# Weight transfers of the expert stage placed behind the second tile's row gathers, and a splitting step, a product and filler work moved to other points of the routing

## The chip, the cores and the metric

The kernel runs on one core of a Trainium2 chip. That core has a matrix engine (TensorE, PE in the profile; its weight loads are listed as PEld), a vector engine (VectorE, DVE), a scalar engine (ScalarE, ACT), a general engine (GpSimd, POOL) and a queue engine (SyncE, SP) that issues most transfers; 16 DMA engines move the data. The metric is device time in microseconds (us) for one execution. The kernel before takes 780.52 us (median of three runs, 780.04 to 780.82).

## The reference

Three layers follow each other. Attention with a threshold: scores below the row's maximum minus `tau` are dropped. Then a mixture of eight experts, one per token, where a token may take over the expert of the token ahead of it. Then a second mixture of four attention experts with a causal mask.

```
scores = q @ k.T / 8; keep scores >= max - tau; x = softmax(scores) @ v          # 4 batches, 8 heads, 576 tokens
logits = x @ w_gate; local = sigmoid(x @ w_local)
for b, s:  e = argmax(logits[b, s]) if s == 0 or local[b, s] < 0.5 else prev_e   # a chain along the tokens
           out[b, s] = softmax(logits[b, s])[e] * (relu(x[b, s] @ w1[e]) @ w2[e])  # w1: 512x1024, w2: 1024x512
out2 = sum over the top 2 of 4 experts of weight * (causal attention of that expert)
```

The expert layer can't start on a token before the chain along all tokens of its batch is known, and rows are then gathered by expert into tiles of 256 or 352 tokens.

## The kernel before

Each engine executes its instructions in the order in which they were written; that order is made by hand. Stage 1 is the attention over 16 pairs of heads. Its order comes from a table of due times: `at(g, f)` puts step `f` at time `g`, where `g = 9 * p` for pair `p`, and the last pair has times of its own. Work of the next stage is hooked into the last pairs by the tables `EARLY` (routing of the first three batches), `TX0` (transposing the rows of the first expert tile) and `S0` (splitting its weights).

A split turns a 128x1024 piece of a weight matrix into a high part (`w1h`, `w2h`, by ACT, or by DVE for the pieces in `DVEH`) and a low part (`w1l`, `w2l`, the difference, by DVE or POOL), so that three matrix products of reduced precision make one of full precision. A tile's weights are eight pieces, 0 to 3 of `w1` and 4 to 7 of `w2`; two pieces come with each 1 MB transfer into a buffer `raw`.

`Route.main` follows stage 1. It ends the routing: a chain of small DVE steps and small matmuls over all tokens, with scans (L709, L713), the inverse list `inv` (L780) that says which row goes to which tile, and behind it the expert list `erow` (L798, L823) and the probability `psel` of the chosen expert (L825 to L837). While that chain runs, `fill(i)` gives PE `FILL[i]` pieces of the first expert tile's products: there are 32 pieces, 16 of the first product (six matmuls of 256 columns, L992) and 16 of the second (three matmuls of 512 columns, L1017). `flush` then writes the evacuations of finished accumulators.

After `inv`, POOL issues three row gathers for tile 1, the second tile (`first`, L1647). After the routing, `moe` resumes. It issues six weight transfers on SP (`load`, L909), each after reading the expert's number from `erow`; then for each of the three row blocks of tile 1 it runs pieces until `LEFT[i]` are left, transposes the block (`tx`, L961) and issues a gather for a later tile. Tile 1 uses the weights of tile 0, so the six transfers are for tile 2 and the first half of tile 3. The accumulator bank of the transpose of block 1 (`py`) stands where the routing had `po`, the product that selects the chosen expert's probability (L815, read at L833).

Of the kernel before, what the change touches and what calls it, by code (L numbers as in the profile page):

```python
# [9 lines left out]
F32 = mybir.dt.float32  # L10
# [3 lines left out]
I32 = mybir.dt.int32  # L14
AF = mybir.ActivationFunctionType
ALU = mybir.AluOpType
# [21 lines left out]
class Events:  # L38
# [4 lines left out]
    def at(self, g, pri, f, *a):  # L43
        self.n += 1
        self.ev.setdefault(g, []).append((pri, self.n, f, a))
# [53 lines left out]
class Consts:  # L99
# [5 lines left out]
    def load(self):  # L105
        self.nc.sync.dma_start(self.t, self.src)
# [6 lines left out]
def stage1(tc, nc, K, qT, qx, kT, vp, tau, wgl, x_dram, L, X, E2, hooks=(), npair=NP):  # L113
    ctx = ExitStack()
    C = ctx.enter_context(tc.tile_pool(name="s1c", bufs=1))
    P1 = ctx.enter_context(tc.tile_pool(name="s1", bufs=2))
    PS = ctx.enter_context(tc.tile_pool(name="s1p", bufs=1, space=PSUM))
    ident = K["ident"]
# [292 lines left out]
    for p in range(npair):  # L411
        g = 9 * p
        at(g - (27 if p < 2 else 21), load, p)
        at(g - (18 if p < 2 else 4.5), load_v, p)
        if p:
            at(g - 17, split_q, p)
        for a in range(2):
            if p:
                at(g - 9 + 2 * a, split_k, p, a)
                at(g - 8 + 2 * a, split_kl, p, a)  # L420
                at(g - 5 + a, split_ql, p, a)
            else:
                at(2 * a - 7, split_k, p, a)
                at(2 * a - 6, split_kl, p, a)
                at(a / 4 - 5.75, split_ql, p, a)
        at(g - 3.5, merge, p)
        for j in range(9):
            for n, f in (("S", scores), ("red", rowmax), ("tau", thresh), ("exp", expo), ("keep", keep), ("tp", tp), ("ev", tp_ev)):
                at(g + W[n][j], f, p, j)
        at(g + W["diag"], diag, p)  # L430
        T = W
        if p == npair - 1:
            T = dict(W, row=(11.3, 14.36), rev=(11.7, 14.7), recip=10.6)
            at(g + 13, norm_last)
            at(g + 14.71, logits_last)
            at(g + 14.75, norm_last)
        for h in range(2):
            at(g + T["tpm"][h], tpm, p, h)
            at(g + T["pmev"][h], tpm_ev, p, h)
            for k in range(5):  # L440
                at(g + T["av"][h], av, p, h, k)
            at(g + T["xt"][h], av_ev, p, h)
            at(g + T["row"][h], rows, p, h)
            at(g + T["rev"][h], rows_ev, p, h)
        at(g + T["keep"][8] + 0.1, sums, p)
        at(g + T["recip"], recip, p)
        if p < npair - 1:
            at(g + T["rev"][1] + 0.1, norm, p)
# [25 lines left out]
class Route:  # L474
# [201 lines left out]
    def main(self, fill, first):  # L676
# [6 lines left out]
        U, mx = self.U, self.mx  # L683
# [12 lines left out]
        def small(o, l, r, stop=True):  # L696
            mm(o, l, r, start=False, stop=stop, skip_group_check=True)
# [60 lines left out]
        pt = px[:, 276:336].rearrange("p (j g b) -> p j g b", j=5, g=3)  # L758
        for j in range(5):
            small(px[:, 276 + 12 * j:288 + 12 * j], O[:, 128 * j:128 * j + 128], sel2.rearrange("p g b -> p (g b)"))  # L760
        fill(6)
        ln3 = W.tile([128, 5, 128], F16, name="ln3")
        for j in range(5):
# [8 lines left out]
        r1 = W.tile([128, 20, NC], F16, name="r1")  # L772
        v.tensor_tensor(r1, K["iota"][:, 2:].unsqueeze(1).to_broadcast([128, 20, NC]),
                        col[:, 0].rearrange("p j b -> p (j b)").unsqueeze(2).to_broadcast([128, 20, NC]), op=ALU.is_equal)
        self.flush()
        pi = px[:, 340:340 + NC]
        for i in range(20):
# [15 lines left out]
        small(pe[:, 32:34], K["b0"][0:32], tf)  # L793
        fill(7)
        erow = C.tile([1, 2 * NT + 1], I32, name="erow")
        tot = W.tile([1, 2], F32, name="tot")
        fl = W.tile([1, NT + 1], F32, name="fl")
        v.tensor_scalar(erow[:, 0:NT], pe[:, 0:NT], 7.0, None, op0=ALU.min)  # L798
        v.tensor_copy(tot, pe[:, 32:34])
        for n, (o, w) in enumerate(((0, PMAX), (PMAX, LMAX))):  # L800
            v.tensor_scalar(fl[:, o:o + w], K["iota"][0:1, 0:w], tot[:, n:n + 1], None, op0=ALU.is_le)
# [7 lines left out]
        v.tensor_tensor(lt[:, 0], lt[:, 0], lt[:, 1], op=ALU.subtract)  # L809
        v.tensor_reduce(lt[:, 1, 0:1], lt[:, 0], axis=AX.X, op=ALU.max)  # L810
        small(pe[:, 40:41], lt[:, 1, 0:1], K["w8"][:, 7:8])

        po = PS.tile([128, 512], F32, name="po", tag="pa")[:, 0:160].rearrange("p (i e) -> p i e", e=8)
        for j in range(5):
            mm(po[:, 4 * j:4 * j + 4], O[:, 128 * j:128 * j + 128], K["ident"][0:32, 0:32],  # L815
               start=(j == 0), stop=(j == 4), skip_group_check=True)
        fill(8)
        self.flush()
        self.M.splits0()
        v.tensor_tensor(fl[:, NT:], fl[:, PMIN:PMIN + 1], fl[:, PMAX + LMIN:PMAX + LMIN + 1], op=ALU.max)  # L820
        v.tensor_tensor(fl[:, NT:], fl[:, NT:], pe[:, 40:41], op=ALU.add)
        v.tensor_scalar(fl[:, NT:], fl[:, NT:], 1.0, None, op0=ALU.min)
        v.tensor_copy(erow[:, NT:], fl)  # L823
        ex = W.tile([128, 20, 8], F32, name="ex")
        v.tensor_tensor(ex, L.rearrange("p j b n -> p (j b) n")[:, :, 0:8],  # L825
                        mx.rearrange("p j b -> p (j b)").unsqueeze(2).to_broadcast([128, 20, 8]), op=ALU.subtract)
        nc.scalar.activation(ex, ex, AF.Exp)
        den = W.tile([128, 20], F32, name="den")
        psel = C.tile([128, 20], F32, name="psel")
        v.tensor_reduce(den, ex, axis=AX.X, op=ALU.add)  # L830
# [6 lines left out]
            v.tensor_copy(psel[64:128, 16 + 2 * i:17 + 2 * i], psel[0:64, 17 + 2 * i:18 + 2 * i])  # L837
        ctx.close()
        self.slot, self.erow, self.psel = slot, erow, psel


def split_chunk(nc, W, src, t, c):
# [74 lines left out]
def moe(tc, nc, K, R, E, M, yg, W, ctx):  # L917
# [32 lines left out]
    def gather():  # L950
        if rows:
            M.fetch(rows.pop(0))
# [18 lines left out]
    def split(t, c):  # L971
        wc[t, c] = split_chunk(nc, E, R.piece(t, c), t, c)
# [73 lines left out]
    def lab(f, *a):  # L1046
        CUR[0] = f.__name__ + str(a)
        f(*a)
# [4 lines left out]
    def load():  # L1053
        if todo:
            load_w(*todo.pop(0))
# [33 lines left out]
                    yield  # L1089

    yield
    M.splits0 = lambda: split(0, 7)
    pieces = start()
    left = 32
    while not M.routed:
# [4 lines left out]
    P2.append(ctx.enter_context(tc.tile_pool(name="mop2", bufs=1, space=PSUM)))  # L1100
    M.last()
    ws, erow, fetch, fetch3, xscale = M.ws, M.erow, M.fetch, M.fetch3, M.xscale
    for _ in range(6):
        load()
    for i in range(3):
        while left > LEFT[i]:
            next(pieces)
            M.flush()
            left -= 1
        lab(tx, 1, i)  # L1110
        gather()
    for _ in pieces:
        M.flush()
    M.flush()
# [74 lines left out]
class Weights3:  # L1189
# [15 lines left out]
    def split(self, r, n, k):  # L1205
        self.nc.scalar.activation(self.h[n][:, k], r, AF.Copy)
        self.nc.vector.tensor_sub(self.l[n][:, k], r, self.h[n][:, k].bitcast(F32))


def stage3(tc, nc, K, ws, xr, fetch, xscale, row, out, nb=B):  # L1210
# [380 lines left out]
    for y in range(2 * nb):  # L1591
# [10 lines left out]
        for h, n in enumerate((5, 10)):  # L1602
# [6 lines left out]

FILL = (2, 1, 4, 2, 1, 1, 2, 3, 0)
EARLY = (60, 123.4, 123.42, 123.44, 123.46, 124.2, 124.25, (124.55, 125), (125.65, 126.1), (126.12, 126.4), 126.7, 127.2, 127.8, 128.4,
         (129.25, 129.55), 129.7, 129.9, (131.58, 131.95), 132, 133, 134.5, 136, 137.5, 139, (141.1, 141.4))
W0 = 129.8
R0 = 141.45
TX0 = ((146.85, 147.25), (147.7, 149.3))
S0 = ((138.5, 140), (140.3, 142), (144.7, 145.3), (147.4, 147.9), (147.5, 148.2), (147.6, 148.5), (148.8, 148.85))
LEFT = (16, 15, 14)
TL = 4  # L1620
POOL = ((0, 0), (0, 1))
DVEH = ((0, 6),)
# [6 lines left out]
def model(tc, cst, qT, qx, kT, vp, tau, wgl, w12, wqk, wv, wo, out):  # L1629
    nc = tc.nc  # L1630
    with ExitStack() as ctx:
# [6 lines left out]
        with ExitStack() as mx, ExitStack() as rx:  # L1638
# [41 lines left out]
                return f  # L1680

            hooks = [(27, lambda *_: R.clear(tc)), *zip(EARLY, rt.early()), (W0, weights0), (R0, rows0)]
            hooks += [*zip(TX0, (tx0(0), tx0(1))), *zip(S0, map(split0, range(7)))]
            stage1(tc, nc, K, qT, qx, kT, vp, tau, wgl, x_dram, L, X, E, hooks)
            R.more(mx.enter_context(tc.tile_pool(name="mr", bufs=1)), 4, 5)
            W = mx.enter_context(tc.tile_pool(name="mo", bufs=1))
# [36 lines left out]

            def last():
                rx.close()
                M.erow = rt.erow
                M.ws = Weights3(tc, nc, ctx, wqk=wqk, wv=wv, wo=wo)

            M.fetch, M.fetch3, M.xscale, M.last = fetch, fetch3, xscale, last
# [71 lines left out]
```

## Time and profile before

| what | value |
|---|---|
| median of the runs | 780.52 us (780.04 to 780.82) |
| the profiled execution | 782.99 us, of which the span from first to last instruction is 781.2 us |
| PE busy | 743.2 us, 95% of the span |
| DVE busy | 547.0 us, 70% |
| ACT busy | 490.1 us, 63% |
| POOL busy | 264.9 us, 34% |
| TensorE clock granted, mean | 0.985 of full speed |

Times in the profile count from the first instruction. The span is 1.8 us shorter than the time of the same execution, and that execution is 2.5 us above the median, so differences are worked out inside the span. Stage 1 ends at about 300 us, the routing runs to about 327 us, and the first product of tile 1 starts at 342.44 us.

### The profile page before, as it was taken

What the parts mean: (1) busy time and instruction counts of PE and PEld (TensorE: products, weight loads), DVE (VectorE), ACT (ScalarE), POOL (GpSimd) and SP (SyncE); (2) the same over time, 40 slices, a digit from 0 to 9 for tenths busy, and PEclk for the clock granted to TensorE, in tenths of its full rate; (3) what the DMA queues carried; (4) which work ended last, traced back from release to release, by engine and by line L of the source; (5) the groups of instructions that cost most, each with busy time, mean ns of one, the idle gap of its engine ahead of it and who ended that gap; (6) DMA issues with size and microseconds to landing.
All of it is one profiled execution on the core that took longest, in us unless ns stands there. A gap on an engine that the chain in (4) does not pass through costs nothing. (4 is left out here: it accounts for less than half of the span.)

```text
span 781.2 us, 14282 instructions
## 1 busy us (share of the span) xinstructions
PE 743.2 (95%) x5100; PEld 630.7 (81%) x5100; DVE 547.0 (70%) x1420; ACT 490.1 (63%) x1019; POOL 264.9 (34%) x385
## 2 busy tenths in 40 slices
PE   4999999999998997799999999999979999999997
PEld 3788887888886776688998898898869888888875
DVE  5988888888888877614456546654337888887891
ACT  3788887888887684213455445554236777777784
POOL 5767777767777970300011001100157000000000
PEclk9999999999999999899999999999989999999999
DMA  8348444443441610562468456701134000000102
GB/s 274 122 141 273 161 119 133 156 129 112 123 120 54 249 43 16 194 250 74 153 227 292 149 208 241 271 27 51 42 100 121 12 15 1 28 28 15 55 29 94
DMA packets 37025, 95.70 MB, mean 123 GB/s; under 512 B 4337, under 2 KB 14065, under 8 KB 32849
## 3 DMA queue, kind: packets, MB, share of 16 engines
q1 hardware_dynamic: 31296, 74.77, 28.2%
q0 software_dynamic: 5648, 19.93, 8.4%
q8 instruction: 42, 0.69, 0.4%
q14 instruction: 39, 0.31, 0.1%
HBM read 75.87 MB, written 18.81 MB: 121 GB/s over the span
## 5 line engine op out<-in xcount | busy, mean ns | idle before, releaser
L253 DVE SCALAR_TENSOR_TENSOR P<-S,nm,E 128x576 f32<-128x576 f32 x144 | 116.1, 815 | 9.7 <-ACT E L240 3.7
L230 DVE TENSOR_REDUCE nm<-S 128x1 f32<-128x576 f32 x144 | 106.5, 754 | 20.0 <-PE S L221 19.2
L240 ACT ACTIVATE E<-S,nm 128x576 f32<-128x576 f32 x144 | 103.8, 746 | 9.8 <-DVE nm L230 9.2
L221 PE MATMUL S<-KK,QS 128*128 128x288 f32 x256 | 84.7, 346 | 11.1 <-DVE QS L200 9.7
L266 PE MATMUL X<-cst,P 128*128 128x128 f32 x576 | 86.7, 278 | 0.9 <-ACT PT L277 0.4
L1647 POOL DMA_INDIRECT xg<-x_dram,inv x22 | 23.4, 1062 | 177.7 <-PE px L961 156.4
L266 PEld LDWEIGHTS X<-cst,P 128*128 128x128 f32 x576 | 67.0, 142 | 16.2 <-issue 7.2
L277 ACT ACTIVATE PT<-X 128x512 f32<-128x512 f32 x128 | 75.0, 600 | 6.3 <-PE X L266 2.2
L992 PE MATMUL acc<-xTh,w1l 128*128 128x352 f32 (+1 forms) x256 | 78.1, 305 | 0.0
L992 PE MATMUL acc<-xTh,w1h 128*128 128x352 f32 (+1 forms) x256 | 77.5, 303 | 0.0
L992 PE MATMUL acc<-xTl,w1h 128*128 128x352 f32 (+1 forms) x256 | 77.4, 302 | 0.0
L984 DVE SCALAR_TENSOR_TENSOR hTl<-acc,hTh 128x352 fp32r<-128x352 f32 (+1 forms) x52 | 30.5, 586 | 66.5 <-ACT hTh L983 66.5
L221 PE MATMUL S<-KL,QS 128*128 128x288 f32 x256 | 73.7, 302 | 0.1
L983 ACT ACTIVATE hTh<-acc 128x352 fp32r<-128x352 f32 (+1 forms) x52 | 26.8, 516 | 73.7 <-PE acc L992 73.7
L1017 PE MATMUL py<-w2h,hTh 128*128 128x512 f32 (+1 forms) x176 | 72.0, 409 | 0.0
L309 PE MATMUL Y<-PT,v 128*64 128x320 f32 (+1 forms) x512 | 70.6, 419 | 0.9 <-ACT PT L277 0.7
L1017 PE MATMUL py<-w2l,hTh 128*128 128x512 f32 (+1 forms) x176 | 70.3, 399 | 0.0
L1017 PE MATMUL py<-w2h,hTl 128*128 128x512 f32 (+1 forms) x176 | 70.0, 398 | 0.0
L221 PEld LDWEIGHTS S<-KK,QS 128*128 128x128 f32 x256 | 49.9, 195 | 12.8 <-ACT KK L180 9.2
L309 PEld LDWEIGHTS Y<-PT,v 128*64 128x64 f32 x512 | 34.3, 138 | 25.9 <-issue 6.1
L221 PEld LDWEIGHTS S<-KL,QS 128*128 128x128 f32 x256 | 50.3, 196 | 0.4 <-DVE KL L189 0.4
L1716 POOL DMA_INDIRECT raw<-yg,slot x18 | 17.5, 974 | 92.5 <-DMA yg<-y 62.6
(372 smaller groups left out, 1987.0 us busy)
## 6 DMA issues: line engine op xcount, KB each, us to landing
raw<-in_w_dram SPq DMA_DIRECT2D x32, 1024.0 KB, 5.3
kraw<-in_kT_dram SPq DMA_DIRECT2D x15, 608.0 KB, 4.1
QS<-in_qT_dram POOLq DMA_DIRECT2D x15, 576.0 KB, 4.1
v<-in_vp_dram SPq DMA_DIRECT2D x16, 320.0 KB, 3.0
qraw<-in_qx_dram SPq DMA_DIRECT2D x16, 288.0 KB, 2.9
yg<-y SPq DMA_DIRECT2D x17, 256.0 KB, 3.4
x_dram<-xr SPq DMA_DIRECT2D x16, 256.0 KB, 2.4
yg<-raw SPq DMA_DIRECT2D x1, 3072.0 KB, 13.5
```

The lines of the kernel that those rows point to most:

```text
L221: nc.tensor.matmul(o, QS[p % NQ][:, a, cs], k[i][:, sl(576 * a)], start=(n == 0), stop=(n == 1))
L230: nc.vector.tensor_reduce(nm[:, 0:1], t[:, :, :288], axis=AX.XY, op=ALU.min)
L240: nc.scalar.activation(e, t[:, :, :288], AF.Exp, scale=-1.0, bias=nm[:, 0:1])
L253: nc.vector.scalar_tensor_tensor(PP[p, c][:, S * a:S * a + S].rearrange("p (h n) -> p h n", h=2), t[:, :, :288], nm[:, 1:2], e, op0=ALU.is ...
L266: nc.tensor.transpose(x[:, 128 * kc:128 * kc + 128], pp[:, o:o + 128], ident)
L277: nc.scalar.activation(PT[p, h][:, a, :, f:f + 128], x.rearrange("p (k q) -> p k q", k=4), AF.Copy)
L309: nc.tensor.matmul(out, l, r, start=s, stop=e, skip_group_check=True)
L983: nc.scalar.activation(hh, p, AF.Relu)
L984: nc.vector.scalar_tensor_tensor(hl, p, 0.0, hh.bitcast(F32), op0=ALU.max, op1=ALU.subtract)
L992: nc.tensor.matmul(o, a[:, fs], x[:, k, 0:w], start=(first and n == 0), stop=(k == 3 and n == 2), skip_group_check=True)
L1017: nc.tensor.matmul(ys[t][u][0:m], h, w[:, 512 * f:512 * f + 512], start=(i == 0 and f == 0 and n == 0), stop=(i == 3 and f == 1 and n == 2))
L1647: nc.gpsimd.indirect_dma_start(out=o, out_offset=None, in_=src.rearrange("b s d -> (b s) d"), in_offset=bass.IndirectOffsetOnAxis(ap=inv, ...
```

## The change

1. In the last pair of stage 1, the first four of the ten scaling steps of `norm_last` go from due time 13 to 14.72, behind the last evacuations.
2. Tile 0's piece 6 is split earlier (due 146.75, before pieces 3 and 4), and pieces 5 and 7 are split in `moe`, piece 5 after the first block of tile 1 and piece 7 after the third.
3. One routing scan (`EARLY` entry 128.4) goes to 127.82, ahead of one step of stage 1.
4. `po` goes from the end of the routing to the place ahead of `fill(6)`; the subtraction and exponential of the probabilities (`ex`) go ahead of the inversion's result.
5. `FILL` gives 1 piece instead of 2 at its first place and 1 instead of 2 ahead of the inversion, so that two more pieces run between the end of the routing and the blocks of tile 1.
6. The tile experts are first written to a tile `er`, and copied into `erow` by `tell` after the third block's transpose and the splits. The six weight transfers are written behind that copy.

```diff
-            at(g + 13, norm_last)
+            at(g + 14.72, norm_last)
...
+        po = PS.tile([128, 512], F32, name="po", tag="pa")[:, 0:160].rearrange("p (i e) -> p i e", e=8)
+        for j in range(5):
+            mm(po[:, 4 * j:4 * j + 4], O[:, 128 * j:128 * j + 128], K["ident"][0:32, 0:32],
+               start=(j == 0), stop=(j == 4), skip_group_check=True)
         fill(6)
...
+        ex = W.tile([128, 20, 8], F32, name="ex")
+        v.tensor_tensor(ex, L.rearrange("p j b n -> p (j b) n")[:, :, 0:8],
+                        mx.rearrange("p j b -> p (j b)").unsqueeze(2).to_broadcast([128, 20, 8]), op=ALU.subtract)
+        nc.scalar.activation(ex, ex, AF.Exp)
         self.flush()
         pi = px[:, 340:340 + NC]
...
-        v.tensor_scalar(erow[:, 0:NT], pe[:, 0:NT], 7.0, None, op0=ALU.min)
+        v.tensor_scalar(er, pe[:, 0:NT], 7.0, None, op0=ALU.min)
...
-        po = PS.tile([128, 512], F32, name="po", tag="pa")[:, 0:160].rearrange("p (i e) -> p i e", e=8)
-        for j in range(5):
-            mm(po[:, 4 * j:4 * j + 4], O[:, 128 * j:128 * j + 128], K["ident"][0:32, 0:32],
-               start=(j == 0), stop=(j == 4), skip_group_check=True)
         fill(8)
         self.flush()
-        self.M.splits0()
...
+        self.tell = lambda: v.tensor_copy(erow[:, 0:NT], er)
...
-    M.splits0 = lambda: split(0, 7)
...
-    for _ in range(6):
-        load()
     for i in range(3):
         while left > LEFT[i]:
             next(pieces)
             M.flush()
             left -= 1
         lab(tx, 1, i)
+        if i == 0:
+            split(0, 5)
         gather()
+    split(0, 7)
+    M.tell()
+    for _ in range(6):
+        load()
...
-FILL = (2, 1, 4, 2, 1, 1, 2, 3, 0)
+FILL = (1, 1, 4, 2, 1, 1, 1, 3, 0)
...
-S0 = ((138.5, 140), (140.3, 142), (144.7, 145.3), (147.4, 147.9), (147.5, 148.2), (147.6, 148.5), (148.8, 148.85))
-LEFT = (16, 15, 14)
+S0 = ((138.5, 140), (140.3, 142), (144.7, 145.3), (147.4, 147.9), (147.5, 148.2), (146.75, 146.76))
+LEFT = (17, 16, 14)
...
-            hooks += [*zip(TX0, (tx0(0), tx0(1))), *zip(S0, map(split0, range(7)))]
+            hooks += [*zip(TX0, (tx0(0), tx0(1))), *zip(S0, map(split0, (0, 1, 2, 3, 4, 6)))]
```

DVE at the end of stage 1, between the two parts of the last pair's logits (`lg`), first before and then now; `raw_72`, `raw_73` and `raw_74` hold weight pieces 2 and 3, 4 and 5, 6 and 7 of tile 0.

```order
L357 TENSOR_TENSOR lg<-Y,rc 128x36
L1672 TENSOR_TENSOR xTPl<-Y,xTPh 128x4x128
L857 TENSOR_TENSOR w1l<-raw_72,w1h 128x1024
L857 TENSOR_TENSOR w2l<-raw_73,w2h 128x1024 x2
L854 CAST w2h<-raw_74 128x1024
L857 TENSOR_TENSOR w2l<-raw_74,w2h 128x1024
L1672 TENSOR_TENSOR xTPl<-Y,xTPh 128x4x128
L357 TENSOR_TENSOR lg<-Y,rc 128x54
```

The same place on DVE now:

```order
L357 TENSOR_TENSOR lg<-Y,rc 128x36
L856 CAST w2h<-raw_74 128x1024
L859 TENSOR_TENSOR w2l<-raw_74,w2h 128x1024
L1677 TENSOR_TENSOR xTPl<-Y,xTPh 128x4x128
L859 TENSOR_TENSOR w1l<-raw_72,w1h 128x1024
L859 TENSOR_TENSOR w2l<-raw_73,w2h 128x1024
L1677 TENSOR_TENSOR xTPl<-Y,xTPh 128x4x128
L357 TENSOR_TENSOR lg<-Y,rc 128x54
```

The two steps on `raw_74` went ahead of the first `xTPl`, and one `w2l` on `raw_73` left this place.

PE at the end of the routing, from the last small matmul to the third block of tile 1, before:

```order
L697 MATMUL prest<-cst,lt 1x1
L815 MATMUL po<-cst,O 128x32 x5
L961 MATMUL px<-cst,xg 128x128 x4
L1017 MATMUL py<-w2h,hTh 128x512
L1017 MATMUL py<-w2l,hTh 128x512
L1017 MATMUL py<-w2h,hTl 128x512
L961 MATMUL py<-cst,xg 128x128 x4
L1017 MATMUL py<-w2h,hTh 128x512
L1017 MATMUL py<-w2l,hTh 128x512
L1017 MATMUL py<-w2h,hTl 128x512
L961 MATMUL px<-cst,xg 128x96 x4
```

The beginning of that place on PE now, to the first block:

```order
L697 MATMUL prest<-cst,lt 1x1
L994 MATMUL acc<-xTPh,w1h 128x256
L994 MATMUL acc<-xTPl,w1h 128x256
L994 MATMUL acc<-xTPh,w1l 128x256
L994 MATMUL acc<-xTPh,w1h 128x256
L994 MATMUL acc<-xTPl,w1h 128x256
L994 MATMUL acc<-xTPh,w1l 128x256
L963 MATMUL px<-cst,xg 128x128 x4
```

The five `po` rows are gone from here, and a piece of the first product stands ahead of the first block; the next piece of it stands ahead of the second block, and two pieces of the second product ahead of the third.

DVE behind the routing now, from the product with `po` on:

```order
L833 TENSOR_TENSOR ex<-po,ex 128x160
L834 TENSOR_REDUCE psel<-ex 128x20
L835 TENSOR_TENSOR psel<-psel,den 128x20
L837 COPY psel<-psel 64x1 x2
L969 TENSOR_TENSOR xTl<-px,xTh 128x4x128
L859 TENSOR_TENSOR w2l<-raw_73,w2h 128x1024
L986 SCALAR_TENSOR_TENSOR hTl<-acc,hTh 128x2x256
L969 TENSOR_TENSOR xTl<-py,xTh 128x4x128
L969 TENSOR_TENSOR xTl<-px,xTh 128x4x96
L859 TENSOR_TENSOR w2l<-raw_74,w2h 128x1024
L841 COPY erow<-er 1x23
```

The copy into `erow`, which SP's first read of an expert number waits for, stands last; before, `erow` was written straight from the matmul, ahead of the whole row list shown here. SP's own list is the same before and now.

## Rows read from the trace of the kernel before

**Rows 1.** Busy time by stretch, 300 to 342 us: stretch, length, each engine, PEclk, DMA share, GB/s.

```profile
300.29:302.95 2.66, 2.65 (x12) 2.58 (x12) 1.35 (x8) 1.53 (x6) 0.14 (x1) 0.52 0.25 71
...
314.40:317.23 2.83, 2.83 (x13) 2.71 (x13) 2.54 (x10) 0.60 (x1) 0.00 (x0) 0.50 0.00 0
...
324.17:330.39 6.22, 1.61 (x9) 0.91 (x8) 3.89 (x16) 1.42 (x3) 1.97 (x2) 0.78 1.00 337
330.39:334.52 4.13, 4.13 (x12) 3.36 (x13) 0.56 (x1) 0.49 (x1) 0.95 (x1) 0.50 1.01 420
334.52:342.44 7.92, 7.92 (x35) 6.38 (x34) 0.00 (x0) 0.60 (x1) 0.00 (x0) 1.00 1.00 410
```

**Rows 2.** Waits, 288 to 345 us: who for whom, us in total, times, longest.

```profile
PE py L961 <- DVE ex L833: 2.6, 1, 2.6
PE acc L992 <- ACT xraw L359: 2.5, 1, 2.5
...
PE px L961 <- DMA xg<-x_dram,inv: 2.0, 1, 2.0
```

**Rows 3.** Timeline, end of stage 1, DVE: start, us, instruction, idle before and releaser.

```profile
292.51 0.69 DVE L1672 TENSOR_TENSOR xTPl<-Y,xTPh 128x512 fp32r<-128x512 f32 x1 [1.90 <-ACT xTPh L1671]
...
294.73 2.35 DVE L857 TENSOR_TENSOR w2l<-raw,w2h 128x1024 fp32r<-128x1024 f32 x2
297.00 0.69 DVE L854 CAST w2h<-raw 128x1024 fp32r<-128x1024 f32 x1
297.73 1.22 DVE L857 TENSOR_TENSOR w2l<-raw,w2h 128x1024 fp32r<-128x1024 f32 x1
...
299.47 0.20 DVE L357 TENSOR_TENSOR lg<-Y,rc 128x54 f32<-128x54 f32 x1
```

**Rows 4.** Timeline, end of stage 1, PE and ACT.

```profile
294.62 0.66 PE L1666 MATMUL Y<-cst,xg 128*128 128x128 f32 x4
...
295.36 1.05 ACT L383 ACTIVATE xr<-xraw,rc 128x64 f32<-128x64 f32 x4
...
296.78 1.01 PE L341 MATMUL Y<-iq,XT 128*128 128x146 f32 x6 [1.51 <-ACT XT L321]
```

**Rows 5.** Timeline, routing, DVE.

```profile
301.64 0.20 DVE L522 TENSOR_TENSOR U<-eq,fr 128x40 bf16<-128x40 f32 x1
...
305.22 1.21 DVE L709 TENSOR_TENSOR_SCAN O<-A,pg 32x512 f32<-32x512 f32 x1 [3.38 <-PE prest L697]
...
306.90 1.35 DVE L713 TENSOR_TENSOR_SCAN R<-cst,O 32x576 f32<-32x576 f32 x1
...
315.81 0.83 DVE L773 TENSOR_TENSOR r<-cst,col 128x640 f16<-128x640 f32 x1
...
318.00 0.19 DVE L780 TENSOR_SCALAR inv<-prest 128x32 int32<-128x32 f32 x1 [0.49 <-PE prest L697]
```

**Rows 6.** Timeline, end of the routing, PE and DVE.

```profile
321.59 1.30 PE L815 MATMUL po<-cst,O 32*128 32x32 f32 x10
...
322.20 0.69 DVE L984 SCALAR_TENSOR_TENSOR hTl<-acc,hTh 128x512 fp32r<-128x512 f32 x1 [1.45 <-ACT hTh L983]
...
323.15 1.23 DVE L857 TENSOR_TENSOR w2l<-raw,w2h 128x1024 fp32r<-128x1024 f32 x1 [0.26 <-ACT w2h L856]
```

**Rows 7.** Tile `xg`: landing of tile 1's three gathers, then of two alone at 281 us.

```profile
DMA to landing us min/median/max: 3.4/5.6/9.2
...
DMA to landing us min/median/max: 3.5/3.5/3.5
```

**Rows 8.** Timeline: tile 1's first gather, the six weight transfers, their first reader.

```profile
318.46 1.04 POOL L1647 DMA_INDIRECT xg<-x_dram,inv  x1 [16.39 <-DVE col L783]
...
320.45 4.29 SPq L909 DMA_DIRECT2D raw<-in_w_dram  x6
...
363.32 2.00 ACT L856 ACTIVATE w1h<-raw 128x1024 fp32r<-128x1024 f32 x2
```

**Rows 9.** Tile `raw`, 320 to 325 us: landing of the six weight transfers.

```profile
DMA to landing us min/median/max: 6.3/15.4/20.2
```

More of the change, by code (lines that the diff above doesn't have):

```diff
@@ L795, in main @@
         erow = C.tile([1, 2 * NT + 1], I32, name="erow")
+        er = C.tile([1, NT], I32, name="er")
         tot = W.tile([1, 2], F32, name="tot")
         fl = W.tile([1, NT + 1], F32, name="fl")
-        v.tensor_scalar(erow[:, 0:NT], pe[:, 0:NT], 7.0, None, op0=ALU.min)
+        v.tensor_scalar(er, pe[:, 0:NT], 7.0, None, op0=ALU.min)
         v.tensor_copy(tot, pe[:, 32:34])
@@ L823, in main @@
         v.tensor_copy(erow[:, NT:], fl)
[L824 to L827, printed above, removed]
         den = W.tile([128, 20], F32, name="den")
@@ L1607, in stage3 @@
     ctx.close()
-FILL = (2, 1, 4, 2, 1, 1, 2, 3, 0)
-EARLY = (60, 123.4, 123.42, 123.44, 123.46, 124.2, 124.25, (124.55, 125), (125.65, 126.1), (126.12, 126.4), 126.7, 127.2, 127.8, 128.4,
+FILL = (1, 1, 4, 2, 1, 1, 1, 3, 0)
+EARLY = (60, 123.4, 123.42, 123.44, 123.46, 124.2, 124.25, (124.55, 125), (125.65, 126.1), (126.12, 126.4), 126.7, 127.2, 127.8, 127.82,
          (129.25, 129.55), 129.7, 129.9, (131.58, 131.95), 132, 133, 134.5, 136, 137.5, 139, (141.1, 141.4))
@@ L1725, in last @@
                 rx.close()
-                M.erow = rt.erow
+                M.erow, M.tell = rt.erow, rt.tell
                 M.ws = Weights3(tc, nc, ctx, wqk=wqk, wv=wv, wo=wo)
```

## The prediction

> **What bounds the kernel now.** I read the busy shares first: PE has work in 95% of the span, so what shortens the run is either less work for PE or fewer gaps and slow stretches in it. The table of slices shows one place where PE is well below full, between stage 1 and the first product of tile 1, and the change edits just that place. I then read its waits by stretch. Before 342.44 us PE waits three times: 2.5 us for `xraw` at the end of stage 1, 2.6 us for the bank of `po` and 2.0 us for a row gather [rows 2]. Beside the waits stand three stretches at the lower of the two clock levels, granted 0.50 to 0.52: 2.66 us with the first filler work, 2.83 us ahead of the inversion, 4.13 us behind the gather [rows 1]. The reader is to see there that each slow stretch follows a time in which PE did little: 9 instructions in the 6.22 us ahead of the last one. At the low level a 256-column matmul takes 0.22 us (2.66 by 12); at the full one a 512-column matmul takes 0.233 us (7.92 by 34, since the first of the 35 had begun earlier), and a 256-column one half of that, 0.117.
>
> After 342.44 us PE is again nearly full, and weights arrive ahead of their use, so a gain made here should stay until the end.
>
> **Tail of stage 1.** DVE is the late engine: it waits 1.90 us for `xTPh`, and then works almost without a break until the second `lg` at 299.47 [rows 3]. Now the cast and the low part of piece 6 (0.69 + 1.22 = 1.91 us) lie in that 1.90 us, and one `w2l` (half of 2.35, 1.17 us) is gone from here. So the last `w2l` ends at 294.73 + 1.17 = 295.9. On ACT one split (1.0 us, half of the 2.00 in [rows 8]) and four scalings (1.05 us) no longer stand ahead of the last `XT`, which had kept PE waiting 1.51 us [rows 4]. XT can start when the matmuls ahead of the transposes of 294.62 are done, and PE can take the last `rows` right behind these transposes, at 295.3, for 1.0 us. `xTPh` (0.6) ends at 296.0, its DVE part (0.7) at 296.7, and `lg` starts there: 2.75 us earlier.
>
> From `lg` to the end of `U` it takes 2.37 us (299.47 to 301.84, [rows 3, 5]), so `U` is there at 299.1. PE's filler ahead of it was 12 matmuls and ended at 302.95, 1.1 us behind `U` [rows 1, 5]; now 6 of them, 0.7 to 1.3 us, begin at 297.5 (0.82 us behind `lg`, as before, [rows 1, 3]) and end ahead of `U`. From the end of the filler to the scan it was 305.22 - 302.95 = 2.27 us [rows 1, 5]. With 0 to 0.6 us more, if the six matmuls of `fill(1)` run at the low level, the scan starts between 301.4 and 302.0. I take 301.7: **3.5 us** gained. The ten scalings that now stand together on ACT (2.6 us, to 300.1) end about as the copy `A` can start; the rows they write are only read by gathers more than ten us later.
>
> **From the scan to the inverse list.** Beside the scans (305.22 to 308.25, 3.03 us, [rows 5]) PE does 24 matmuls: 2.8 us at the full level, 5.3 at the low one. Before, the low stretch was over by then. Now PE comes to them earlier, with less work behind it, and the clock may still be low: this costs 0 to 2.2 us, and I take **0.5 lost**: a slow stretch as long as the old ones holds twelve matmuls [rows 1], some of them in `fill(1)`; eight left over here lose 0.8 us, of which the scans, 0.25 us longer than the matmuls, hide a part. In `fill(6)` six matmuls (1.36 us at the low level) make place for `po`, 1.30 us [rows 6]; the DVE side is ready 0.6 us ahead of PE there (316.64 against 317.23, [rows 1, 5]), so this is worth 0.05 to 0.6; I take **0.1**. The early `ex` on DVE lies in the 1.36 us between the end of `r` and `inv` [rows 5], in place of a longer step that moves behind `inv`: nothing. `inv` then comes 3.1 us earlier, at 314.9.
>
> **From the inverse list to tile 1's product**, counted from `inv` (318.00 before). PE was done with `po` at +4.9; without it +3.6 [rows 6]. One piece, 0.7: +4.3. The first gather is issued at +0.46 and lands 3.4 us later, at +3.9 [rows 7, 8], so block 1 doesn't wait: +4.8. Another piece: +5.5. Block 2 needs the bank of `po`. The `hTl` in that chain waited 1.45 us for ACT [rows 6]; it is now that of the group before, so it starts at 322.20 - 1.45, +2.75. From its start to the release it took 4.57 us (to 324.17 + 2.6, [rows 1, 2]); the `w2l` and its wait (1.23 + 0.26) leave the chain, which gives +5.8, or up to 0.7 less with the exponential done. Gather 2 lands at +5.2 if it takes 3.5 us. So block 2 ends at about +6.3, two pieces of the second product (1.4) at +7.7, block 3 (gather 3 at +6.5) at +8.2, and the other 14 pieces (42 x 0.233 = 9.8) at +18.0. Before it was 342.44 - 318.00 = +24.4: 6.4 us. As a cross-check: two waits of 2.6 and 2.0, and half of the 4.13 us at the low level [rows 1, 2], make 6.7. Here too clock may be lost: `fill(7)` and the two pieces are 30 matmuls, 0 to 3.2 us. I take 0.9: **5.5 gained**.
>
> That the gathers take 3.5 us is the assumption behind this. Tile 1's took 3.4, 5.6 and 9.2 us; the first landed as the weight stream began (320.45), and two with nothing beside them took 3.5 each [rows 7, 8]. With the weights behind `tell` all three are alone.
>
> **The weights.** `tell` stands behind the low part of piece 7: block 3's evacuation (about 1.2), a split of 1.0 and 1.23 from +8.2 give +11.6. Before, the first transfer came 2.45 us behind `inv` (318.00 to 320.45, [rows 5, 8]), with the writing of `erow` in between; SP's read and issue are less than that, and I take one us. So it starts at +12.6: 10 us later. The six take 4.3 us to issue [rows 8], to +16.9; behind them on SP stand tile 0's stores, which are due only as tile 1's product starts, at +18. The last landed 20.2 us behind its issue [rows 9]: at worst +37. Their first reader is ACT's split at 363.32 [rows 8], 20.9 us behind tile 1's start, now at +38.9, and it needs only the first two (6.3 us for the fastest, [rows 9]). Cost taken: nothing; cover about 20 us for the first, 2 for the last, which isn't needed until a tile later.
>
> The Trainium skill's page "Trainium Kernel Development and Optimization", section Best Practices, speaks against this edit: overlap transfers with compute, so start them early. By it the 10 us would be a loss; the rows give them about 20 us of cover, so I don't follow it, but it is the third rival.
>
> **The moved scan** is half as long as the one of 1.35 us in [rows 5], 0.7 us. It changes places with other DVE work: -0.7 to +0.7, taken as 0. The copy of `er` is one tiny DVE step: nothing.
>
> **Sum.** 3.5 - 0.5 + 0.1 + 5.5 = 8.6 us. Against the profiled execution's own 782.99 us this is 774.4; that execution lies 2.5 us above the median of the runs, so the forecast is 780.52 - 8.6 = **771.9 us**.
>
> **Rivals.**
> - *The clock stays low longer* (0.14). PE's filler is thinner now: six matmuls instead of twelve at two places, and ten small `po` instructions beside the ten of `sel2`. For it: each thin time before was followed by a low stretch [rows 1]. Against it: PE no longer idles for 2.5, 2.6 and 2.0 us. With both clock charges at their upper ends (2.2 for 0.5, 3.2 for 0.9) the gain is 4.6: 775.9. The Trainium skill's page "TensorE: Matmul & The Clock Gate", section Part 4: PE-mode transpose, says that transposes don't count as busy for the clock. By that rule this rival would be the case, since the blocks of tile 1 are transposes; the low stretch from 330.39 agrees, as most of the nine instructions ahead of it are such.
> - *The gathers are slow by themselves* (0.06): three behind each other, not the weights, make 9.2 us. Then gather 3 lands at 0.46 + 2.6 + 9.2 = +12.3, block 3 waits 4.6 us, and the gain is 4.0: 776.5. Against it stand the two of 3.5 us; for it, that only two were in flight there.
> - *The weights come too late* (0.06): ACT's split of tile 2 waits for the first two transfers, and PE behind it. It decides from 26 us of landing on (+38.9 less +12.6); the longest seen was 20.2. At twice that, 40.4, the wait is 14 us and the time 786: slower. A wait of 7 to 10 us would just give the gain back.
> - The forecast itself has the rest, 0.74.
>
> **Numbers.** No clock charge at all, 0.6 for `fill(6)` and the moved scan in its favour give a gain of 11.2, 769.3; the first two rivals end at 776.5. With a little beyond either end for what no row shows, the range is 768.5 to 777.0. About 1.6 us, 0.2%, is what a measurement can tell. Forecast and the first two rivals are faster; the third is split between slower and no change: faster 0.94, within 0.2% 0.03, slower 0.03.
>
> **What would show it.** In the new profile the second `lg` starts nearly 3 us earlier; `inv` at about 315; PE's waits for `xraw` shorter, those for `ex` and for `xg` gone or under half a us; tile 1's gathers land in 3 to 5 us; the weights start some 12 us behind `inv`; no PE wait behind ACT's first split of tile 2; tile 1's first product at about 333.8. I am wrong if `xg` still lands in 9 us, if the granted clock stays near 0.5 through the second product, or if PE gets a new wait after tile 1.

## The result and the profile after

The changed kernel takes 774.05 us (median of four runs, 772.73 to 775.34) against 780.67 us (780.04 to 780.96) for the kernel before, timed on the same chip: ratio 0.9916, 95% interval 0.9898 to 0.9934. Forecast were 771.9 us, range 768.5 to 777.0. Timed twice more in the comparisons below, beside other runs of the kernel before, it took 772.28 us (ratio 0.9898, 0.9882 to 0.9915) and 773.37 us (0.9899, 0.9882 to 0.9917). So the gain is 6.6, 9.0 and 7.6 us in three comparisons, 7.7 on average; forecast were 8.6.

The busy shares of the page say little: PE has 737.9 us in a shorter span, 96% instead of 95%.

The windows, from the end of stage 1 to tile 1 (the columns as in [rows 1]):

```profile
296.90:302.00 5.10, 3.44 (x29) 2.79 (x29) 3.31 (x13) 3.61 (x13) 0.14 (x1) 1.00 0.21 57
302.00:306.20 4.20, 4.20 (x38) 3.98 (x36) 3.63 (x11) 0.60 (x1) 0.00 (x0) 1.00 0.01 3
306.20:311.50 5.30, 5.09 (x41) 4.59 (x39) 4.49 (x23) 0.60 (x1) 0.00 (x0) 1.00 0.01 3
311.50:314.70 3.20, 1.92 (x32) 1.63 (x31) 2.29 (x11) 0.34 (x1) 0.70 (x1) 0.73 0.00 0
314.70:319.70 5.00, 5.00 (x27) 4.73 (x24) 2.65 (x16) 0.60 (x1) 3.18 (x4) 0.50 0.56 147
...
323.00:333.20 10.20, 10.20 (x48) 8.23 (x47) 3.44 (x6) 2.33 (x4) 1.14 (x2) 1.00 0.70 246
```

Of the three stretches at the lower clock level in [rows 1] one is left, in another place. Finer windows show that it begins just ahead of `inv` (313.53), in the small matmuls of the inversion, and that the 1.0 us in which PE then waits for `q` come after it has begun:

```profile
312.50:313.00 0.50, 0.25 (x9) 0.19 (x8) 0.49 (x2) 0.00 (x0) 0.00 (x0) 0.94 0.00 0
313.00:313.50 0.50, 0.49 (x19) 0.39 (x15) 0.00 (x0) 0.34 (x1) 0.00 (x0) 0.50 0.00 0
```

It lasts to about 319.8, so all of `fill(7)`, from 314.71, lies in it. The fillers of the first stretch and the second product run at the full level. From the first `lg` to tile 1 the clock stands at the lower level for about 7 us, where it was about 14 in the kernel before.

PE's waits from 280 to 345 us:

```profile
PE acc L994 <- ACT xraw L359: 1.1, 1, 1.1
PE prest L697 <- DVE q L799: 1.0, 1, 1.0
PE prest L697 <- ACT A L707: 0.5, 1, 0.5
```

The 2.6 us for `ex` and the 2.0 us for `xg` of [rows 2] are gone, the 2.5 us for `xraw` are 1.1.

DVE's timeline, to be laid beside [rows 3, 5]; the times are later by whatever the run lost earlier, so differences count, from the first `lg` on:

```profile
291.14 0.20 DVE L357 TENSOR_TENSOR lg<-Y,rc 128x36 f32<-128x36 f32 x1 [0.64 <-PE Y L341]
...
297.28 0.20 DVE L357 TENSOR_TENSOR lg<-Y,rc 128x54 f32<-128x54 f32 x1
...
299.46 0.20 DVE L522 TENSOR_TENSOR U<-eq,fr 128x40 bf16<-128x40 f32 x1
301.14 1.21 DVE L709 TENSOR_TENSOR_SCAN O<-A,pg 32x512 f32<-32x512 f32 x1 [1.48 <-ACT A L706]
...
313.53 0.19 DVE L789 TENSOR_SCALAR inv<-prest 128x32 int32<-128x32 f32 x1 [0.55 <-PE prest L697]
...
326.29 0.16 DVE L841 COPY erow<-er 1x23 int32<-1x23 int32 x1
```

Tile 1's first product starts at 333.27. The landing of its gathers, then SP's six weight transfers with their landing, then ACT's first split of tile 2:

```profile
DMA to landing us min/median/max: 3.5/3.6/4.9
```

```profile
327.46 3.95 SPq L911 DMA_DIRECT2D raw<-in_w_dram  x6
```

```profile
DMA to landing us min/median/max: 4.8/9.6/14.2
```

```profile
354.15 2.00 ACT L858 ACTIVATE w1h<-raw 128x1024 fp32r<-128x1024 f32 x2
```

The gathers that took 3.4, 5.6 and 9.2 us [rows 7] take under 5. The weights start 13.9 us behind `inv` (forecast 12.6), and ACT's split still doesn't wait (nothing stands in brackets behind it); it starts 20.9 us behind tile 1's first product, as before.

One thing got worse, 50 us earlier, in stage 1. DVE with the moved scan (L584, its second half), POOL at the same time (and, in the first row, at the same step of an earlier pair), and PE, in the changed kernel:

```profile
250.63 0.91 DVE L584 TENSOR_TENSOR_SCAN R<-cst,O 24x288 f32<-24x288 f32 x1
251.47 0.18 DVE L235 TENSOR_SCALAR nm<-nm,taut 128x1 f32<-128x1 f32 x1
251.58 1.81 DVE L584 TENSOR_TENSOR_SCAN R<-cst,R,O 24x288 f32<-24x288 f32 x1
253.31 0.78 DVE L253 SCALAR_TENSOR_TENSOR P<-S,nm,E 128x576 f32<-128x576 f32 x1
```

```profile
231.38 1.43 POOL L192 TENSOR_TENSOR KL<-kraw,KK 128x576 fp32r<-128x576 f32 x1
...
250.27 0.68 POOL L191 TENSOR_SCALAR kraw<-kraw 128x576 f32<-128x576 f32 x1
251.03 1.75 POOL L192 TENSOR_TENSOR KL<-kraw,KK 128x576 fp32r<-128x576 f32 x1
```

```profile
254.16 0.40 PE L221 MATMUL S<-KK,QS 128*128 128x288 f32 x1 [1.58 <-DVE P L253]
```

The scan takes 1.81 us, its first half of the same size 0.91, and PE waits 1.58 us for the `P` that stands behind it. The two other profiled executions of the changed kernel (c0 and d0 below) show the same wait of 1.6 us; in the kernel before PE doesn't wait for `P` there.

### The profile page after: what moved, and what is told of

Its sections match the earlier page's. It is cut to its first block, busy times and chain, and to the rows that moved or that the text cites. A ratio compares the mean times of both kernels' runs of the same rounds, so it can differ in the third digit from the quotient of the medians.

```text
span 772.4 us, 14282 instructions
## 1 busy us (share of the span) xinstructions
PE 737.9 (96%) x5100; PEld 627.8 (81%) x5100; DVE 548.7 (71%) x1421; ACT 490.3 (63%) x1019; POOL 264.6 (34%) x385
## 5 line engine op out<-in xcount | busy, mean ns | idle before, releaser
L240 ACT ACTIVATE E<-S,nm 128x576 f32<-128x576 f32 x144 | 103.8, 746 | 13.1 <-DVE nm L230 12.6
L221 PEld LDWEIGHTS S<-KK,QS 128*128 128x128 f32 x256 | 49.6, 194 | 15.3 <-issue 12.6
```

What stands on the lines that cost most here:

```text
L221: nc.tensor.matmul(o, QS[p % NQ][:, a, cs], k[i][:, sl(576 * a)], start=(n == 0), stop=(n == 1))
L240: nc.scalar.activation(e, t[:, :, :288], AF.Exp, scale=-1.0, bias=nm[:, 0:1])
```

## The experiments

Each was timed in five rounds beside the kernel before; kernels of one comparison ran on the same chip (A: before 780.13 us; B: 781.27; C: 781.0). The changed kernel itself is in B and C and not in A, so what undoing a part costs in A is read from the traces and from the ratios to the kernel before. Beside the medians I use two pieces of each profiled run: the *stage-1 piece*, from DVE's reciprocal (L333) at 199 us to the first `lg` of the last pair, which holds the moved scan; and the *edited piece*, from that `lg` to tile 1's first product. Before, they are 91.3 and 52.0 us, changed 91.5 and 42.1. The later stretch from tile 1 to the last evacuation of `y` in the expert stage is 215.9 to 216.3 us in every kernel: what is gained ahead of tile 1 isn't given back there.

**a1: only the late weights** (the kernel before with item 6 of the change). Comparison A.

```diff
-        v.tensor_scalar(erow[:, 0:NT], pe[:, 0:NT], 7.0, None, op0=ALU.min)
+        v.tensor_scalar(er, pe[:, 0:NT], 7.0, None, op0=ALU.min)
...
-    for _ in range(6):
-        load()
     for i in range(3):
...
+    M.tell()
+    for _ in range(6):
+        load()
```

> The kernel before with one part of the change alone: the expert list is copied by `tell` behind the third block, and the six weight transfers stand behind it; splits, `po`, fillers and scaling stay as before. My theory: the three gathers of tile 1 land in 3.5 to 5 us instead of 3.4, 5.6 and 9.2, PE's wait of 2.0 us for `xg` goes, the wait of 2.6 us for `po`'s bank stays, and some of the 4.13 us at the low clock goes with the shorter gap: 777 to 778.5 us. Rival (the gathers are slow by themselves, one behind the other): the third still lands in about 9 us and the time is 780.5 us, as before.

Measured: 777.98 us, ratio 0.9975 (0.9957 to 0.9992); edited piece 49.4. PE's waits of [rows 2], 280 to 345 us:

```profile
PE py L964 <- DVE ex L834: 2.6, 1, 2.6
PE acc L995 <- ACT xraw L359: 2.5, 1, 2.5
PE Y L341 <- ACT XT L321: 1.5, 1, 1.5
```

The wait for `xg` is gone, the others stand as they were. So starting the weights later is by itself worth 2.6 us in the edited piece and 2.2 in the medians (0.6 to 3.4 by the ratio's interval), and ACT's first split of tile 2 doesn't wait for them. The landing of the gathers is not in this trace; the wait alone shows that they came sooner.

**a2: the weights early again** (changed kernel, `erow` written directly, four transfers back ahead of the blocks). Comparison A.

```diff
+    for _ in range(4):
+        load()
...
-    M.tell()
-    for _ in range(6):
+    for _ in range(2):
         load()
```

> The changed kernel with the expert list written straight into `erow` and the first four of the six weight transfers back ahead of the three blocks (the other two, whose buffers the splits of pieces 5 to 7 still read, stay behind them). My theory: gathers 2 and 3 land in 5 to 9 us again, block 3 waits about 2.5 us for its rows, and PE works at the low clock for some us behind that gap: 776.5 to 778.5 us. Rival (the gathers don't care for the weights): block 3 doesn't wait, 774 us, as the changed kernel.

Measured: 776.65 us, ratio 0.9954 (0.9938 to 0.9970); edited piece 46.3. PE's longest wait:

```profile
PE px L960 <- DMA xg<-x_dram,inv: 2.4, 1, 2.4
```

The wait for the gather comes back with the weights, though it is the same three gathers in the same order. The third gather was issued at 315.18, and block 3 was released at 324.35, 9.2 us later, where the changed kernel's gathers take 4.9 at most. This answers the rival of gathers slow by themselves: the weight stream beside them is what made them slow. In the whole change the late weights are worth more than alone, 4.2 us by the traces and 3.0 to 4.4 by the ratios. The clock has a part in it: the edited piece of a2 holds about 10 us at the lower level, that of the changed kernel about 7.

**a3: the splits as before** (changed kernel, items 1 and 2 undone). Comparison A.

```diff
-            at(g + 14.72, norm_last)
+            at(g + 13, norm_last)
...
-        if i == 0:
-            split(0, 5)
-    split(0, 7)
...
-S0 = (..., (147.5, 148.2), (146.75, 146.76))
+S0 = (..., (147.5, 148.2), (147.6, 148.5), (148.8, 148.85))
```

(Piece 7 is also split at the end of the routing again, as in the diff of the change.)

> The changed kernel with the splits of tile 0's pieces 5 to 7 and the first four scalings of `norm_last` back at their old places. My theory: DVE's second `lg` comes 2.2 to 3 us later, PE stands still ahead of the first filler again, the clock is low for it, and the `w2l` of piece 7 is back in the chain ahead of the product with `po`: the inverse list some 3.5 to 4.5 us later and 777 to 779 us. Rival (the split is hidden anyway, and the gain came from the gathers and `po`): 774 to 775 us.

Measured: 776.29 us, ratio 0.9948 (0.9930 to 0.9966); edited piece 46.6; 777 to 779 us were expected. PE's waits:

```profile
PE acc L995 <- ACT xraw L359: 2.5, 1, 2.5
PE Y L341 <- ACT XT L321: 1.5, 1, 1.5
```

From the first `lg` to the second it is 9.06 us, as before, instead of 6.14, and from there to the scan 5.4 instead of 3.9. In the traces the splits and scalings carry 4.5 of the 4.8 us that the change gains ahead of the scan; by the ratios they are worth 2.5 to 3.9 us.

**a4: product, `ex` and fillers as before** (changed kernel, items 4 and 5 undone). Comparison A.

```diff
-FILL = (1, 1, 4, 2, 1, 1, 1, 3, 0)
+FILL = (2, 1, 4, 2, 1, 1, 2, 3, 0)
...
-LEFT = (17, 16, 14)
+LEFT = (16, 15, 14)
```

(`po` also goes back behind `fill(7)`, and `ex` behind the flush, as in the diff of the change.)

> The changed kernel with `po`, the exponential `ex`, and the filler counts (FILL, LEFT) back as before; splits, scaling, scan and transfers stay changed. My theory: PE does `po` (1.3 us) between the last filler and block 1 again, its bank is released later, so block 2 waits 1 to 2 us; ahead of the chain 12 matmuls instead of six delay the routing by 0.5 to 1.3 us, while the fuller PE keeps its clock up, which gives back up to 2 us: 774.5 to 776.5 us. Rival (the thinner fillers only cost clock): 772 to 773.5 us, faster than the changed kernel.

Measured: 773.69 us, ratio 0.9914 (0.9894 to 0.9934). My theory had 774.5 to 776.5: missed. In the profile the edited piece is 44.1, 1.9 us longer, and PE waits for `ex` again; in the ratios (0.9914, against 0.9916, 0.9898 and 0.9899 for the changed kernel) 0 to 1.2 us are lost. By itself this was inconclusive, and a9 asks again.

**a5 and c5: only the scan as before** (changed kernel, `EARLY` entry 127.82 back to 128.4), in comparisons B and C, and **c0 and d0: the changed kernel again** beside them.

```diff
-EARLY = (..., 127.2, 127.8, 127.82,
+EARLY = (..., 127.2, 127.8, 128.4,
```

> The changed kernel with one part undone: the second half of the early routing scan back at due time 128.4. In the new profile that scan takes 1.81 us instead of 0.91, beside POOL's 1.75 us subtraction, and PE waits 1.6 us for the step of stage 1 behind it. My theory: back in its old place it takes 0.91 us, PE doesn't wait, and the kernel is 1 to 1.6 us faster than the changed one: 772.3 to 773.2 us. Rival (it costs nothing, since DVE's work is only permuted, as I put it in the prediction): 774 us.

> The changed kernel, unchanged, beside the others on this chip: 773.5 to 774.5 us, and from the first `lg` to tile 1's first product about 42 us again, less up to 2 if the low stretch in `fill(7)` falls elsewhere.

> The changed kernel with only the scan as before, again. If the moved scan costs what the two traces differ by, this is 1 to 2.5 us under the changed kernel timed beside it, at 770 to 771.5. If the first 770.7 was the spread of the runs, it lies within 0.7 us of the changed kernel.

> The changed kernel as it is, timed beside the three others. Expected: 772 to 774.5, ratio to the kernel before 0.988 to 0.993, and 42.0 to 42.3 us from the first logits to tile 1. Outside of that the difference of 1.6 us to the kernel with the old scan can't be told from spread.

Measured in B: 770.68 us, ratio 0.9863 (0.9846 to 0.9879), against the changed kernel's 772.28, 0.9898 (0.9882 to 0.9915). In C: 770.86 us, 0.9870 (0.9854 to 0.9887), against 773.37, 0.9899 (0.9882 to 0.9917). So this version beats both kernels; in the medians undoing this one item is worth 1.6 and 2.5 us. In B the fastest run of the changed kernel (772.11) is slower than the slowest of a5 (770.89); in C the two overlap. Three expectations were missed: a5 was faster than 772.3, c0 faster than 773.5, and the edited piece of d0 is 43.2 us, not 42.0 to 42.3 (c0: 42.0). DVE and POOL in the run of c5, at the place shown above for the changed kernel:

```profile
250.38 0.82 DVE L253 SCALAR_TENSOR_TENSOR P<-S,nm,E 128x576 f32<-128x576 f32 x1
251.12 0.09 DVE L253 DVE_READ_ACCUMULATOR P<-S,nm,E 128x1 f32 x1
251.12 0.75 DVE L230 TENSOR_REDUCE nm<-S 128x1 f32<-128x576 f32 x1
251.79 0.91 DVE L584 TENSOR_TENSOR_SCAN R<-cst,R,O 24x288 f32<-24x288 f32 x1
```

```profile
249.65 1.76 POOL L192 TENSOR_TENSOR KL<-kraw,KK 128x576 fp32r<-128x576 f32 x1
251.37 0.73 POOL L178 TENSOR_SCALAR KK<-kraw 128x640 fp32r<-128x640 f32 x1
```

Here POOL's subtraction is over when the scan starts, the scan takes 0.91 us, and `P` stands ahead of it.

The stage-1 piece needs care, because a low clock at 255 to 261 us comes and goes in it from one execution to the next, in both kernels. Sorted by both:

| | full clock at 255 to 261 us | lower level in part of it |
|---|---|---|
| scan at its old place | 89.9 (before again, a1, a9) | 91.3 to 91.4 (before, a5, c5, a8, a10) |
| scan moved | 91.5 (changed, c0, a2) | 91.7 (a3), 92.0 (d0), 93.3 (a4) |

Two executions with the scan at its old place, first c5 and then a9, show the two columns (windows):

```profile
255.00:258.00 3.00, 3.00 (x16) 1.39 (x14) 2.90 (x16) 0.65 (x2) 2.84 (x3) 0.56 0.27 41
258.00:261.00 3.00, 3.00 (x21) 2.02 (x18) 1.91 (x6) 1.03 (x2) 2.38 (x4) 0.88 0.87 355
```

```profile
255.00:258.00 3.00, 3.00 (x23) 1.50 (x22) 2.83 (x19) 1.25 (x3) 2.84 (x4) 1.00 0.12 16
258.00:261.00 3.00, 2.96 (x23) 2.55 (x21) 2.86 (x10) 1.54 (x4) 2.92 (x5) 1.00 0.88 330
```

At full clock, like against like, the moved scan costs 1.6 us, which is PE's wait of 1.58. At the lower level the difference is 0.3 to 0.7 us (a3 and d0; the low stretch of a4 is about twice as long as the others). The profiled executions of a5 and c5 fell into the right column and that of the changed kernel into the left one, so their stage-1 pieces look alike, 91.4 and 91.5, though the wait is gone: only the table separates the two causes.

**b0: the kernel before, profiled again** (no change).

> The kernel before, unchanged, for a second profile of it. My theory: the profiled execution of before (782.99 us) lies above its runs by chance, through the lengths of stretches at the low clock that the change doesn't touch; here the parts from the first `lg` of the last pair to tile 1's first product again take about 52 us (51 to 53), and the rest sums to less: 779 to 781 us. Rival: those 52 us were themselves the outlier, and this profile shows 49 to 50.

Measured: 780.26 us (a single execution), stage-1 piece 89.9, edited piece 52.0. The edited piece is the same to 0.05 us in two executions of the kernel before. In three of the changed kernel it is 42.1, 42.0 (c0) and 43.2 (d0), so a gain of 8.8 to 9.9 us there is not spread.

**a9: a4 with the scan as before.** Comparison C, beside c5.

```diff
-EARLY = (..., 127.2, 127.8, 127.82,
+EARLY = (..., 127.2, 127.8, 128.4,
...
-FILL = (1, 1, 4, 2, 1, 1, 1, 3, 0)
+FILL = (2, 1, 4, 2, 1, 1, 2, 3, 0)
...
-LEFT = (17, 16, 14)
+LEFT = (16, 15, 14)
```

> The changed kernel with the moved scan and also the product with po, ex, FILL and LEFT as before, so loads and splits alone. If po and fill pay what the traces of the edited stretch showed (2.0 us), this is 1.5 to 2.5 us above the kernel that has only the scan as before: about 772.7, and the time from the first logits to tile 1 is 43.5 to 44.5 us, PE waiting about 1.1 us for ex again. If po and fill are worth nothing at the end, as the medians had it, it is within 0.7 us of 770.7 and the stretch is 41.5 to 42.5 us.

Measured: 771.36 us, ratio 0.9885 (0.9867 to 0.9903), against c5's 770.86; edited piece 43.1 against 41.7. PE's waits:

```profile
PE acc L994 <- ACT xraw L359: 1.1, 1, 1.1
PE py L963 <- DVE ex L833: 1.1, 1, 1.1
```

Of the two expectations the time fits the second and the edited piece lies between them. The profiles give 1.4 us to product and fillers, but c0 and d0, which are one program, differ by 1.2 there; the medians give 0.5 with intervals that overlap. What they are worth at the end stays open between 0 and about 1.5 us.

**a8 and a10: one filler piece elsewhere** (a5 with another `FILL`), in B and C.

```diff
-FILL = (1, 1, 4, 2, 1, 1, 1, 3, 0)
+FILL = (1, 1, 4, 2, 1, 1, 2, 2, 0)    # a8: two pieces ahead of the inversion, two behind
...
-FILL = (1, 1, 4, 2, 1, 1, 1, 3, 0)
+FILL = (1, 1, 4, 3, 1, 1, 0, 3, 0)    # a10: three pieces earlier, none ahead of the inversion
```

> The changed kernel with the scan in its old place and one piece moved from `fill(7)` to `fill(6)`, ahead of the inversion (FILL 1,1,4,2,1,1,2,2,0). My theory: PE is done with `fill(6)` 0.5 us later than the DVE side, so the inverse list comes 0.4 to 0.5 us later; PE has more to do ahead of `fill(7)`, and if that keeps its clock up there, 12 to 18 matmuls are 0.1 us shorter each: 771.5 to 773 us, within half a us of the version with the scan alone. Rival (the clock drops there all the same): 772.8 to 773.7 us, slower than that version by the later inverse list.

> The changed kernel with the scan as before, and the one piece ahead of the inversion's result (fill 6) moved to the place of fill 3 (three pieces there instead of two). If the low clock around the inversion takes its price from the filler in front of the chain, the inverse list comes 1.0 to 1.4 us earlier (11.5 to 11.9 us behind the scan instead of 12.8), of which the low clock behind it may take back some: 769.5 to 770.5. If the thinner work only brings the low clock earlier, the list comes no sooner than 12.6 us behind the scan and the time is 770.7 to 773.

Measured: a8 772.67 us (0.9875, 0.9853 to 0.9898) against a5's 770.68; a10 771.58 us (0.9884, 0.9868 to 0.9899) against c5's 770.86. Neither is better in the median. But the five runs of a8 form two groups, 769.4 (twice, mean granted clock 0.993 and 0.994) and 772.7 to 773.0 (three times, 0.987 to 0.989), and the profiled one is of the slower group: its trace tells of that group alone. From the scan to `inv` it is 15.0 us in a8, 2.2 more than the 12.8 of a5, where 0.4 to 0.5 more were expected; in a10 it is 13.1, against 12.7 in c5. The windows around `inv`, first of a8 (`inv` at 315.02), then of a10 (312.77):

```profile
308.00:311.00 3.00, 2.97 (x22) 2.83 (x22) 2.72 (x16) 0.00 (x0) 0.00 (x0) 0.83 0.00 0
311.00:314.50 3.50, 3.31 (x32) 3.10 (x32) 0.95 (x3) 0.93 (x2) 0.00 (x0) 0.50 0.00 0
```

```profile
310.00:313.20 3.20, 1.57 (x29) 1.44 (x28) 2.54 (x13) 0.34 (x1) 0.00 (x0) 0.90 0.00 0
313.20:318.20 5.00, 4.43 (x24) 4.15 (x24) 2.59 (x16) 0.60 (x1) 3.89 (x4) 0.50 0.43 129
```

The low stretch isn't avoided in either trace. In a8 it covers the filler ahead of `inv`, on which the routing's chain waits. In a10 the filler is gone, yet `inv` comes no sooner.

## Why the prediction was right, step by step

**Tail of stage 1: right.** Forecast: the second `lg` 2.75 us earlier. Measured from the first `lg`: 9.06 before, 6.14 after, 2.92. a3 takes it back whole.

**From `lg` to the scan: too small.** Forecast was 0.75 more (3.5 in all), measured 1.9 (5.75 to 3.86). The step that failed is the place from which the 2.27 us were counted. The forecast had the filler end ahead of `U`, and counted from the end of `U`, with 0.3 on top for a low clock in `fill(1)`. In the trace the 2.27 hold from the end of the filler, as before: 298.92 to 301.14 is 2.22. PE's first product behind the filler, `pa`, needs only the half of `U` that L516 writes, 1.26 us ahead of the half that L522 writes at 299.46; and what ends last ahead of the scan is ACT's copy `A`, behind the ten scalings. The changed kernel:

```profile
298.20 0.18 DVE L516 TENSOR_SCALAR U<-fr 128x40 bf16<-128x40 f32 x1
299.05 0.40 PE L701 MATMUL pa<-identb,U 128*32 128x128 bf16 x4
300.52 0.59 ACT L706 ACTIVATE A<-pa 32x512 f32<-32x512 f32 x1
```

So the 1.9 us are those of the filler: twelve matmuls took 2.67 us at the low level, six take 0.81 at the full one. a4 has twelve there at the full level and 4.27 us from `lg` to the scan, so about 1.5 of the 1.9 us are the clock and 0.4 the thinner filler.

**From the scan to `inv`: too careful, in two executions of three.** Forecast was a net loss of 0.4 (0.5 for the clock, 0.1 back); measured a gain of 0.4 (12.78 to 12.39, and 12.38 in c0), since the lower level began only 0.6 us ahead of `inv`. In d0 it began some 2 us earlier, and there 0.7 us were lost (13.45).

**From `inv` to tile 1: gathers and waits right, clock too small.** Forecast 5.5, measured 4.7 (24.44 to 19.74). The waits for `ex` and `xg` went and the gathers took 3.5 to 4.9 us, as said. But `fill(7)` ran at the low level: its 18 matmuls took 4.0 us (from 314.71), at 0.117 us each they are 2.1; three more of the next piece add 0.4. So the charge was 2.3 us where I took 0.9, within the 0 to 3.2 that I gave. The lower clock turned up in a new place: it began in the matmuls of the inversion, at about 312.9, instead of in the blocks of tile 1.

**The edited piece** gained 9.9 us (52.0 to 42.1; 8.8 in d0), forecast 8.6. By an estimate from the time at the lower level (about 14 against 7 us, and a matmul takes twice as long there) at most 3.4 of the 9.9 us are the clock.

**The moved scan: wrong.** I costed it at 0, with 0.7 us either way, because it "changes places with other DVE work". It lost 1.6. It was also sized too small, at 0.7 us for half of another scan, where its own row in the trace of the kernel before has 0.91:

```profile
252.63 0.91 DVE L584 TENSOR_TENSOR_SCAN R<-cst,R,O 24x288 f32<-24x288 f32 x1
```

Two things were left out. Ahead of `P` it delays a step that PE waits for, where before it ran behind `P`. And it now starts while POOL's subtraction with two operands in memory is running: 1.81 us instead of 0.91. The trace shows the two overlapping from 251.58 to 252.78, the scan ending 0.6 us behind POOL, and c5 shows both undone by one due time. By an estimate 0.90 of PE's 1.58 us are the longer scan and the rest its place. The Trainium skill's page "SBUF — State Buffer", section "SBUF: two separate sides", says that VectorE and GpSimd share one pair of ports as an exclusive lock, against a GpSimd operation that reads SBUF for a VectorE operation with two inputs in SBUF as well, and that the one that starts first keeps it for its whole instruction. The trace agrees in kind: the scan's first half, which started first, kept its 0.91, and the subtraction that started during it took 1.75 instead of 1.43; the second half, which started during the subtraction, lost 0.90. In size it doesn't quite: a scan that had to wait for the whole subtraction would end 0.91 us behind it, not 0.6. That the ports are the cause is argued from this overlap; no run here separates them from another cause.

**Sum.** 9.9 - 1.6 = 8.3 at like clock in the stage-1 piece, against 8.6 forecast and 7.7 on average in the medians. Against the forecast the terms came out 0.2, 1.1 and 0.8 us better (tail, `lg` to the scan, scan to `inv`) and 0.8 and 1.6 worse (`inv` to tile 1, the moved scan). That they nearly cancel is luck: the total is better than its terms. The rest of the distance from 771.9 to 774.05 us is no larger than what executions differ by where the change touches nothing: the start (198.2 to 199.6 us), and the stretch behind the last evacuation of `y` (220.5 to 223.2).

**The rivals.** *Gathers slow by themselves*: out, by a2 and by the landing times. *Weights too late*: out, by the split at 354.15 without a wait, and a1. The Trainium skill's page "Trainium Kernel Development and Optimization", section Best Practices, asks that transfers overlap with compute; that the later start would therefore be a loss was the prediction's conclusion from it. Here it is 2.6 to 4.2 us of gain in the edited piece, since the transfers delayed are not the next ones needed. *The clock stays low longer*: its charge in `fill(7)` came in part, the one ahead of `inv` only in d0. Two readings of [rows 1] behind this rival don't hold. Ahead of the middle low stretch PE was not idle: from 308 to 314 us it was busy for 5.6 of 6.0. And the last one began at about 327.7 and not at 330.39; the 0.78 in the row ahead of it is a mean of both levels. The prediction took from the Trainium skill's page "TensorE: Matmul & The Clock Gate", section Part 4: PE-mode transpose, that transposes don't count as busy, so that a low stretch would follow the blocks of tile 1 (320.13 to 323.4). The granted clock is 1.00 from 323.00 on, so the trace doesn't bear it out here; the twelve transposes take about 1 us among full matmuls, so it is a weak test.

## What to carry to other kernels

A transfer that isn't needed soon should start behind the small ones that are: the same three gathers took up to 9.2 us beside 1 MB transfers and up to 4.9 without them. A step that only changes places on one engine has a price too: look at who waits for the step it now precedes, and at what the neighbouring engine is doing at that moment. A chain is counted from the step that its first link needs, which here was half of `U` and not the whole. When a term is read from a stretch at the lower clock, write the clock beside it, and cost it at both levels.

## What the runs showed that I had not expected

- The lower clock level is not a fixed property of a place in the program. At 255 to 261 us it came in 8 of 14 profiled executions, in the kernel before once in two, and cost about 1.4 us there (89.9 against 91.3).
- It moves rather than goes. With the waits of [rows 2] gone it came at the next thin place, and d0, the same program as the changed kernel, had it about 2 us earlier than c0, ahead of `inv` (13.45 us from scan to `inv` instead of 12.38), and for about 10 us instead of 7:

```profile
311.15:314.35 3.20, 3.11 (x31) 2.85 (x30) 1.52 (x6) 0.34 (x1) 0.00 (x0) 0.50 0.00 0
```

- A VectorE scan of 24x288 elements took 1.81 us instead of 0.91 when it started during a GpSimd subtraction of 128x576.
